# A sparse attention and a gated FFN in one kernel: the written-out order of its work is replaced behind the first FFN product

## The chip, the cores and the metric

The kernel runs on one NeuronCore of a Trainium2 chip. The metric is the device time of one execution in microseconds (us), as the median of several runs. A profile of one further execution shows what each engine did: PE (TensorE, the matrix engine; PEld its weight loads), ACT (ScalarE), DVE (VectorE), POOL (GpSimd) and SP (SyncE, which here only issues transfers).

## What is computed

```python
# q, k, v: 4 batches, 8 heads, 768 positions, 64 per head
k_sum = k.reshape(B, H, nb, block, D).max(axis=3)        # block = 32
v_sum = v.reshape(B, H, nb, block, D).mean(axis=3)
scores_l = scale * np.matmul(q, k.transpose(0, 1, 3, 2)) # kept where |i - j| < 16
scores_s = scale * np.einsum('bhsd,bhnd->bhsn', q, k_sum) + np.log(block)
# softmax over both together, then the weighted sum over v and v_sum
x = attn_out.transpose(0, 2, 1, 3).reshape(B * S, H * D) # 3072 tokens, 512 wide
h = x @ w_in                                             # 512 -> 2048
g = h * np.clip(h + 3.0, 0.0, 6.0) / 6.0
out = g @ w_out                                          # 2048 -> 512
```

## The kernel before

The tokens are cut into eight tiles of 384, numbered s = 2 x batch + half. A tile's x is made by the attention of that half batch; then come the first FFN product (512 -> 2048, in eight pairs of 128 rows), a gate on ScalarE and VectorE, and the second FFN product (2048 -> 512, for three groups of 128 tokens).

All work is cut into some 785 small jobs, and `ORDER` is a text that lists them, one token each. A token names a job as *group.number*, and a letter behind a colon picks ScalarE (A) or VectorE (D) where either can do it. Every engine carries out its own tokens strictly in the order of the text. `Plan.run` walks through the text, gives each job a begin and an end by fixed costs, hands out buffers by them (so the text also decides which buffer a job gets), and puts the jobs of all engines out by their planned begin. Waits between engines are set from what the jobs read and write.

The tokens that matter here:

- `F{s}{c}`: first FFN product of tile s. `.0`, `.1` and `.4`, `.5` are TensorE jobs of four products each (line 928), `.2`, `.6` the ScalarE part of the gate (934), `.3`, `.7` the VectorE part (936). A pair of products holds one of three PSUM tiles `S` until its VectorE part is done.
- `G{s}{t}`: second FFN product of 128 tokens. `.0` to `.3` are TensorE jobs of four products (950), `.4` a copy into one of four output buffers `ot` (517), `.5` the store (964, 965), on SP's queue but for G51. A buffer is free again when its store has landed.
- `s{b}{k}`: scores of batch b (681): a TensorE job, an exponential on ScalarE, a mask on VectorE.
- `u{b}`: sums of v by blocks (752) and the copies that spread them over `vaug`.
- `v{b}{T}`: attention values, in two TensorE jobs of 24 products (841), with a scaling on VectorE behind each. For tiles 2, 4, 5, 6 and 7 the last job, `.6`, is a DMA transpose on SP's queue (854) that writes the tile's x; it is called a *turn* below.
- `K`, `Q`, `V`, `h{b}0` to `h{b}2`, `B`: loads on GpSimd's software DMA queue. `I` and `O` load the weights. The raw K and Q of batches 1 and 2 are transposed by VectorE (`k{b}{p}`, `q{b}{p}`, lines 612 and 618); those of batch 3 by turns on SP's queue (`k3e0`, `k3e1`, `q3x0`, `q3x1`, lines 594 and 603).
- `h{b}{c}{x}` of batch 1: the halo of v, a copy within `vaug` (521).
- `y10`: one copy of two elements on GpSimd that reads tile 2's x. GpSimd does nothing more before that turn has landed.

The two lines that make `y10` what it is:

```python
            if b == 1:
                plan.at(f"y{b}{half}")
                op("POOL", 0.15, lambda: nc.gpsimd.tensor_copy(seen[0:1], xt[s].slot[0:1, 0, 0, 0:2]), r=[xt[s], ("x", s, 0)], w=["seen"])
```

Of the kernel before, what the change touches and what calls it, by code (L numbers as in the profile page):

```python
# [38 lines left out]
K10.0 v00.4 u03.1:A v03.0 v00.5:A v03.3 v02.2 v01.4 v02.3 v03.1 v02.4 I3.0 K12.0 K13.0 v01.5:D F00.0 F00.1 v03.2 v02.5:A
F00.2 F00.3 F00.4 v03.4 K11.0 v03.5 F00.5 v03.6 F01.4 F00.6 v03.7:D F01.5 F01.6 F00.7 F00.8 v03.10 v03.8 F00.9 v03.11:A O0.0  # L40
F02.0 v03.9:A F02.1 F01.7 F02.2 F00.10 F00.11 F00.12 F02.3 F00.13 F01.0 F01.1 O1.0 F10.0 F00.14 F10.1 F01.2 F00.15 F01.3
F10.2 F10.3 F13.4 O2.0 F13.5 F13.0 F13.6 F13.1 F11.4 F13.7 F13.2 Q11.0 F11.5 c.3 F12.0 F13.3 Q13.0 F12.1 F11.6 F11.0 F11.7
Q10.0 F11.1 F12.2 F11.2 Q12.0 F03.0 F03.1 F12.3 F03.2 k13.0 F11.3 F02.4 F02.5 F03.3 F02.6 G01.0 k12.0 F10.4 F10.5 k11.0 G01.1
F12.4 F02.7 F12.5 O3.0 k10.0 F03.4 F03.5 F10.6 F10.7 G10.0 w1.0 w1.4:A w1.3:A F12.6 V12.0 G02.0 G02.1 G02.2 F03.6 V10.0 V13.0
F12.7 F03.7 w1.1 q10.0 q13.0 G11.0 G10.1 q12.0 q11.0 G10.2 G11.1 G01.2 h121.0:D w1.2:A G11.2 h120.0:A q14.0:D V11.0 G11.3
h100.0:D h101.0:D G11.4:A G10.3 h130.0:D h131.0:D s120.0 G10.4:A G11.5 s110.0 s120.1 G02.3 G01.3 G00.0 h21.0 G02.4:A h110.0:D
# [6 lines left out]
F20.1 G31.1 F20.2 G32.1 G32.2 F20.3 F21.0 q21.0 F21.4 q20.0 w2.4:A F21.5 F21.1 F20.4 w2.0 F21.6 F21.2 G31.2 G32.3 q22.0 V20.0
F20.5 G32.4:A F21.7 F20.6 F23.0 F23.1 w2.1 G31.3 w2.2:A F20.7 V22.0 G30.0 F21.3 h22.0 G30.1 F23.2 K31.0 s240.0 F23.3 s230.0
s250.0 G30.2 h30.0 G31.4:A s240.1 F22.0 F22.1 B33.0 G30.3 s250.1 s230.1 F22.2 V21.0 u2.0 q24.0:A s210.0 s220.0 F22.3 s200.0
G30.4:A s210.1 s240.2 s220.1 u2.1:D u2.8:D s250.2 s210.2 u2.2:D u2.9:A u2.4:A s230.2 s220.2 u2.7:D G20.0 F22.4 F22.5 F22.6
# [4 lines left out]
k3e1.0 q3x1.0 G31.5 G20.5 F42.4 F42.5 F42.6 F42.7 F50.0 F50.1 F52.4 F52.5 F50.2 F52.6 F50.3 F52.7 G22.4:D F51.4 F51.5 F50.4
F50.5 F51.6 F51.7 F50.6 F50.7 F43.0 F43.1 F43.2 F53.0 F43.3 w3.0 G41.0 F51.0 F53.1 F53.2 F53.3 F51.1 F53.4 F53.5 F51.2 F53.6
G41.1 w3.1 F43.4 F53.7 F51.3 F43.5 F43.6 F43.7 U3.1 w3.4:D w3.3:D G41.2 F52.0 G40.0 F52.1 G40.1 G41.3 G40.2 G40.3 F52.2
w3.2:D G41.4:D F52.3 G40.4:A s350.0 s300.0 s320.0 s300.1 s320.1 U3.4:A s350.1 u3.7:A u3.6:A G50.0 G50.1 G52.0 G52.1 s310.0
s340.0 s330.0 G52.2 G52.3 G50.2 s310.1 s340.1 u3.4:A u3.2:A s330.1 u3.0:D s300.2 s350.2 s320.2 u3.1:D s310.2 u3.3:D u3.5:D
v33.0 v33.3 G52.4:D G51.0 G51.1 v33.4 v33.1 v33.2 s340.2 v33.5 G42.0 G42.1 G51.2 G51.3 G42.2 s330.2 v30.0 v30.1 v30.2 v30.3
v30.4 v30.5 G42.3 G52.5 G41.5 G22.5 v33.6 F70.0 F70.1 F70.2 G51.4:A F71.0 F71.1 F71.2 G42.4:D v30.6 G51.5 F70.3 F71.3 F71.4
F71.5 F71.6 F71.7 F70.4 F70.5 F72.4 F72.5 F70.6 F70.7 F60.0 F60.1 F63.4 F63.5 G50.3 F60.2 F60.3 F63.6 F72.6 F63.7 F61.0 F61.1
F72.7 G72.0 F61.2 F73.4 F73.5 F73.6 G50.4:A F61.3 F73.7 F72.0 F72.1 F72.2 F72.3 F73.0 F73.1 F63.0 G71.0 F61.4 F63.1 F61.5
F73.2 F73.3 F63.2 F63.3 G71.3 F61.6 F61.7 F62.4 F62.5 F62.0 G71.1 G71.6 F62.6 F62.7 G71.9 G72.1 G71.4 G72.2 G71.7 F60.4 F62.1  # L70
G71.12 G71.13:A F60.5 G72.3 G70.0 G70.1 G70.2 F60.6 F60.7 F62.2 F62.3 G60.0 G60.1 G70.3 G61.0 G71.14 G42.5 G70.4:D G60.2
G72.4:D G70.5 G72.5 G60.3 G60.4:D G60.5 G71.10:D G71.11 G40.5 G50.5 G62.0 G62.1 G62.2 G61.1 G61.2 G61.3 G62.3 G61.4:D G61.5
G62.4:D G62.5 G71.2 G71.5 G71.8 G71.15 G71.16:A G71.17
# [1023 lines left out]
```

## Time and profile before

| | |
|---|---|
| median of three runs | 212.12 us (211.94 to 213.3) |
| the profiled execution | 211.65 us |
| its span, first to last instruction | 209.9 us |
| granted TensorE clock, mean | 0.999 |
| busy: PE, DVE, ACT, POOL | 201.7, 156.0, 110.8, 68.9 us |
| software DMA queue (GpSimd's loads) | 15.47 MB in 99488 packets |
| hardware DMA queue (SP's turns and stores) | 10.06 MB in 18128 packets |

Times in the profile count from the span's start. A row of a timeline gives start, length, engine, line of the kernel, operation, the tiles written and read with their shapes, and how many instructions were merged; a bracket tells how long the engine was idle before and who ended that. TensorE's products overlap, so the sum of their lengths is more than the time that they take; starts are the better ruler. A few products in a hundred have no record.

### The profile page before, as it was taken

How to read it: one execution, taken by the hardware profiler on the slowest of the kernel's cores; microseconds unless marked ns; L12 is line 12 of the kernel's file. 1: busy time of each engine (PE TensorE's matmuls, PEld its weight loads, DVE VectorE, ACT ScalarE, POOL GpSimd, SP SyncE). 2: the span in 40 equal slices, each digit the busy share in tenths (PEclk: the TensorE clock that was granted, in tenths of full speed). 3: DMA queues.
4: the chain of work that ended last, by engine and by line, in shares of the span. 5: the costliest groups of instructions: out<-in, count | busy, mean ns of one | idle time of the engine just before them, and what ended most of it. 6: DMA issues, size and time to landing. Idle time of an engine off the chain costs nothing.

```text
span 209.9 us, 5030 instructions
## 1 busy us (share of the span) xinstructions
PE 201.7 (96%) x2143; PEld 119.1 (57%) x2166; DVE 156.0 (74%) x229; ACT 110.8 (53%) x158; POOL 68.9 (33%) x89
## 2 busy tenths in 40 slices
...
GB/s 143 198 160 189 165 152 131 204 135 152 158 159 157 124 110 199 137 164 160 161 169 38 173 132 208 214 24 0 2 54 174 67 61 0 3 0 62 23 185 182
DMA packets 117638, 25.85 MB, mean 123 GB/s; under 512 B 108368, under 2 KB 114320, under 8 KB 117616
## 3 DMA queue, kind: packets, MB, share of 16 engines
q0 software_dynamic: 99488, 15.47, 106.8%
q1 hardware_dynamic: 18128, 10.06, 20.3%
q8 instruction: 17, 0.28, 0.6%
q14 instruction: 5, 0.04, 0.1%
...
## 4 chain that ended last, share of the span: by engine, by line
PE 60%; DMA 22%; POOL 5%; issue 5%; DVE 5%; ACT 2%; SPq 0%; POOLq 0%; ACTq 0%
PE S L928 28%; PE h L950 19%; PE S L950 9%; DMA vaug<-in_v_dram 9%; DMA wout<-in_moe_w_out_dram 5%; DMA win<-in_moe_w_in_dram 4%; DMA g<-in_q_dram 3%; PE S L841 2%; POOL nat L455 2%; DMA out_dram<-ot 2%; DVE at L689 2%; DVE g L936 1%; PE S L681 1%; DVE vaug L517 1%; ACT at L687 1%
## 5 line engine op out<-in xcount | busy, mean ns | idle before, releaser
L928 PE MATMUL S<-x,win 128*128 128x384 bf16 (+1 forms) x616 | 87.8, 299 | 0.4 <-ACT ot L517 0.3
L936 DVE SCALAR_TENSOR_TENSOR g<-r,S 128x768 bf16<-128x768 f32 x64 | 59.9, 948 | 24.5 <-ACT r L934 24.2
L934 ACT ACTIVATE r<-S 128x768 f32<-128x768 f32 x64 | 51.1, 810 | 46.0 <-PE S L928 42.0
L928 PEld LDWEIGHTS <-win 128*128 128x128 bf16 x616 | 53.6, 98 | 31.6 <-issue 0.8
L950 PEld LDWEIGHTS <-g 128*128 128x128 bf16 x416 | 38.7, 98 | 40.3 <-DVE g L936 0.4
L950 PE MATMUL h<-wout,g 128*128 128x512 bf16 (+2 forms) x256 | 58.6, 362 | 1.5 <-issue 1.0
L950 PE MATMUL S<-wout,g 128*128 128x512 bf16 (+1 forms) x139 | 30.0, 361 | 0.6 <-issue 0.3
L965 POOL DMA_DIRECT2D out_dram<-ot x1 | 0.6, 586 | 59.0 <-ACT ot L517 59.0
L687 ACT ACTIVATE at<-S 120x1024 bf16<-120x1024 f32 x18 | 17.9, 1023 | 1.6 <-PE S L681 1.4
L467 POOL DMA_DIRECT2D vaug<-in_v_dram x16 | 15.2, 949 | 6.4 <-issue 5.7
L517 ACT COPY ot<-h 128x512 f32<-128x512 f32 (+1 forms) x12 | 6.7, 558 | 18.4 <-PE h L950 16.9
L689 DVE TENSOR_TENSOR at<-at,mask 96x1024 bf16<-96x1024 bf16 x18 | 11.7, 683 | 1.6 <-ACT at L687 0.9
L455 POOL DMA_DIRECT2D nat<-in_k_dram x8 | 10.5, 1319 | 6.2 <-issue 4.7
L455 POOL DMA_DIRECT2D nat<-in_q_dram x8 | 10.6, 1329 | 3.3 <-issue 2.7
L782 DVE TENSOR_REDUCE red<-kb 128x48 bf16<-128x1536 bf16 x6 | 10.4, 1738 | 0.0
L517 DVE COPY ot<-S 128x512 f32<-128x512 f32 x5 | 3.5, 690 | 9.0 <-PE S L950 5.8
L517 ACT COPY ot<-S 128x512 f32<-128x512 f32 (+1 forms) x4 | 2.0, 502 | 14.8 <-DMA out_dram<-ot 10.0
L618 DVE STREAM_TRANSPOSE q<-nat 128x768 bf16<-128x768 bf16 x8 | 7.3, 956 | 2.8 <-issue 2.8
L521 DVE TENSOR_TENSOR vaug<-vaug 32x640 bf16<-32x640 bf16 (+2 forms) x21 | 7.7, 409 | 1.6 <-DMA vaug<-in_v_dram 1.2
L517 ACT COPY vaug<-vs 24x768 bf16<-24x768 bf16 x10 | 8.2, 827 | 0.2
L849 DVE TENSOR_TENSOR xm<-S,rc 128x768 bf16<-128x768 f32 x8 | 7.6, 954 | 0.2
L739 DVE TENSOR_REDUCE total<-nat 128x32 f32<-128x1024 bf16 x4 | 7.6, 1897 | 0.0
...
## 6 DMA issues: line engine op xcount, KB each, us to landing
...
wout<-in_moe_w_out_dram POOLq DMA_DIRECT2D x4, 512.0 KB, 11.4
nat<-in_q_dram POOLq DMA_DIRECT2D x8, 192.0 KB, 13.6
...
```

Source lines behind the costliest of these rows:

```text
L455: op("POOL", 1.35, over=0.01, fn=lambda src=src, name=name, hs=hs, ds=ds, rows=rows: nc.gpsimd.dma_start(out=raw[b % 2][name][rows], in_=s ...
L467: op("POOL", 0.945, lambda: nc.gpsimd.dma_start(out=o[BLK:WIN, lo:hi, 0:D], in_=rows[:, lo:hi]), w=[("v", b % 2, c)], dma=1.28, els=1536). ...
L517: {"ACT": nc.scalar.copy, "DVE": nc.vector.tensor_copy, "POOL": nc.gpsimd.tensor_copy}[eng](o, i)
L521: nc.vector.tensor_tensor(o, i, i, op=ALU.max)
L687: op("ACT", 1.02, lambda: nc.scalar.activation(odds[0:KEYS, :, w], X.slot[0:KEYS], AF.Exp, scale=scl), r=[X], w=[("atg", k)])
L689: op("DVE", 0.69, lambda: nc.vector.tensor_tensor(odds[0:WIN, :, w].rearrange("p j (t c) -> p j t c", c=QB), odds[0:WIN, :, w].rearrange(" ...
L739: nc.vector.tensor_reduce(total[:, h * D + lo:h * D + lo + n], x[:, lo:lo + n], axis=AX.X, op=ALU.add)
L782: nc.vector.tensor_reduce(red.slot[:].rearrange("x (p u e n) -> x e u p n", p=NP, u=NS, e=2)[:, e], w[:, n * e:n * e + n, BLK:WIN].rearran ...
L928: nc.tensor.matmul(h.slot[:, f, u * 128:z * 128].rearrange("p (u c) -> p u c", c=128), w_in_sb[:, kt, (ft + f) * 128:(ft + f + 1) * 128], ...
L934: op("ACT", 0.81, lambda: nc.scalar.activation(r.slot[:], h.slot[:, :, 0:HALF], AF.Relu, bias=0.5, scale=1.0 / 6.0), r=[h], w=[r], alloc=r)
L936: op("DVE", 0.955, lambda: nc.vector.scalar_tensor_tensor(gt[s].slot[:, ft:ft + 2], r.slot[:], 1.0, h.slot[:, :, 0:HALF], op0=ALU.min, op1 ...
L950: nc.tensor.matmul(bank(o)[:, a:z], gt[s].slot[:, ft, ts * 128:(ts + 1) * 128], w_out_sb[:, ft, a:z], start=(ft == 0), stop=(ft == NFT - 1))
```

## The change

Only `ORDER` changes, from token 123 of 785 on, which is shortly before the first FFN product. It is a new order of the same jobs: 28 of them go to the other one of ScalarE and VectorE, none is added or left out. The costs in `Plan` are as before. Some stretches of it (each line holds many tokens; lines left out are marked):

```diff
-m.0 s110.1 G01.4:A s100.0 s150.0 s100.1 h111.0:D u1.0 u1.1:A K20.0 u1.6:A Q23.0 K22.0 s130.0 G00.1 G00.2 G00.3 Q21.0 K21.0
...
-v10.0 v10.3 Q22.0 v13.9:D G02.5 v10.1 F30.0 v10.2 F30.1 F30.2 v10.4 v10.5 v10.6 F30.4 F30.5 F31.4 F30.3 F31.5 G10.5 F30.6
-G12.4:A F33.4 G12.5 F30.7 F31.6 F33.5 y10.0 G01.5 F33.6 k21.0 F31.7 F33.0 F33.7 F33.1 h20.0 G31.0 Q32.0 F33.2 V30.0 F32.0
-k20.0 F31.0 F33.3 F31.1 F31.2 k22.0 F32.1 F32.4 k23.0 F32.2 F32.5 F31.3 q23.0 G32.0 F32.6 Q33.0 F20.0 w2.3:A F32.3 F32.7
...
-F23.4 G22.0 F23.5 G20.1 G22.1 F22.7 u2.3:D u2.6:D F23.6 F23.7 s200.1 v20.0 v20.3 s200.2 v20.4 v20.1 u2.5:D v20.2 v20.5 B31.0
-K32.0 Q35.0 h31.0 K35.0 K33.0 Q31.0 V32.0 K34.0 B32.0 B30.0 h32.0 V31.0 Q34.0 Q30.0 V33.0 G21.0 G21.1 G22.2 G22.3 v23.3 v23.0
-G20.2 G20.3 G21.2 G21.3 v20.6 G30.5 G21.4:A U3.2 v23.1 v23.4 U3.3 v23.2 U3.0 v23.5 F40.0 F40.1 F40.2 F41.4 F41.5 F41.6 F40.3
...
+h110.0:D m.0 G00.1 s100.1 s100.2 h111.0:A s110.1 s120.2 u1.0 u1.1:A u1.9:D u1.7:D s110.2 u1.3:D G02.4:A s130.0 K23.0 s150.0
...
+F31.0 F31.1 Q20.0 k21.0 F32.6 F32.3 v10.6 G32.0 F32.7 F20.0 k23.0 F31.2 F21.4 F31.3 w2.0 w2.1 F21.5 K30.0 F20.1 F21.6 F20.2
+F20.3 F21.7 Q22.0 q23.0 h21.0 G32.1 G32.2 w2.3:D V21.0 w2.2:A F20.4 F20.5 G32.3 G32.4:A G32.5 F21.0 q20.0 Q32.0 w2.4:A F20.6
...
+F22.0 G30.4:D u2.2:A Q34.0 F23.6 G22.1 u2.6:A s200.2 k3e0.0 F22.7 u2.7:A G20.0 v20.3 F23.7 v20.0 v20.4 v20.1 v20.2 F22.1
+k3e1.0 F22.2 G20.1 G21.0 v20.5 B30.0 B33.0 F22.3 G21.1 G21.2 G21.3 v20.6 G20.2 G20.3 G21.4:A u2.5:D w3.3:A s220.2 v23.3 G21.5
+B31.0 w3.0 w3.1 v23.0 v23.1 v23.2 G20.4:A F40.0 F40.1 F40.2 v23.4 v23.5 F42.0 F42.1 F42.2 F41.4 F41.5 F40.3 F42.3 F41.6 F41.0
...
+G72.3 G71.6 G71.9 G62.1 G72.4:A G72.5 G71.10:A G60.5 G71.11 G62.2 G62.3 y10.0 G71.2 G71.5 G71.8 G62.4:D G61.4:A G62.5 G61.5
...
```

GpSimd's queue, behind the third input weight, in the two orders (loads by their group names):

```
before  K10 I3 K12 K13 K11 O0 O1 O2 Q11 Q13 Q10 Q12 O3 V12 V10 V13 V11 h21 m K20 Q23 K22 Q21 K21 K23 K30 Q20 V23 Q22
        y10 h20 Q32 V30 Q33 V20 V22 h22 K31 h30 B33 V21 B31 K32 Q35 h31 K35 K33 Q31 V32 K34 B32 B30 h32 V31 Q34 Q30 V33
after   K10 I3 K12 K13 O0 K11 O1 Q13 O2 Q12 Q10 Q11 O3 V12 V13 V10 V11 m K23 K22 K20 Q21 V20 K21 h20 Q30 Q23 V22 K33
        K32 Q20 K30 Q22 h21 V21 Q32 K35 h22 V23 K34 K31 Q31 h30 B32 Q34 B30 B33 B31 h31 Q33 Q35 V32 h32 V31 V30 V33 ... y10
```

SP's queue, from batch 1's values on: before, two stores, the turn of tile 2, the stores of G10, G12 and G01, the turn of tile 4, G30 and G00, the turn of tile 5, then the Q and K turns of batch 3 with stores between them. After: the stores of G01, G12 and G02, the turn of tile 2, the stores of G32, G31, G00 and G11, the two K turns of batch 3 and behind them the turn of tile 4, G21, G30, the turn of tile 5, G20, and the Q turns of batch 3.

More of the change, by code (lines that the diff above doesn't have):

```diff
@@ L38 @@
 u03.0:A h031.0:D u02.1:A h021.0:A I0.0 v01.0 v00.0 v00.1 v01.1 u02.2:D v00.2 I1.0 I2.0 v00.3 v02.0 v01.2 v02.1 u01.1:A v01.3
[L39 to L46, printed above, removed]
@@ L47 @@
-m.0 s110.1 G01.4:A s100.0 s150.0 s100.1 h111.0:D u1.0 u1.1:A K20.0 u1.6:A Q23.0 K22.0 s130.0 G00.1 G00.2 G00.3 Q21.0 K21.0
-s120.2 s100.2 u1.3:D u1.5:D u1.2:D s130.1 u1.7:A u1.9:D s110.2 s130.2 G12.0 v13.3 v13.0 v13.4 s150.1 K23.0 s140.0 v13.1 v13.2
-v13.5 u1.8:A K30.0 Q20.0 s140.1 G12.1 G12.2 v13.6 G12.3 s150.2 u1.4:A v13.7:A V23.0 s140.2 v13.10 v13.8 v13.11:D G00.4:A
-v10.0 v10.3 Q22.0 v13.9:D G02.5 v10.1 F30.0 v10.2 F30.1 F30.2 v10.4 v10.5 v10.6 F30.4 F30.5 F31.4 F30.3 F31.5 G10.5 F30.6
-G12.4:A F33.4 G12.5 F30.7 F31.6 F33.5 y10.0 G01.5 F33.6 k21.0 F31.7 F33.0 F33.7 F33.1 h20.0 G31.0 Q32.0 F33.2 V30.0 F32.0
@@ L52 @@
-k20.0 F31.0 F33.3 F31.1 F31.2 k22.0 F32.1 F32.4 k23.0 F32.2 F32.5 F31.3 q23.0 G32.0 F32.6 Q33.0 F20.0 w2.3:A F32.3 F32.7
[L53 to L56, printed above, removed]
@@ L57 @@
-F23.4 G22.0 F23.5 G20.1 G22.1 F22.7 u2.3:D u2.6:D F23.6 F23.7 s200.1 v20.0 v20.3 s200.2 v20.4 v20.1 u2.5:D v20.2 v20.5 B31.0
-K32.0 Q35.0 h31.0 K35.0 K33.0 Q31.0 V32.0 K34.0 B32.0 B30.0 h32.0 V31.0 Q34.0 Q30.0 V33.0 G21.0 G21.1 G22.2 G22.3 v23.3 v23.0
-G20.2 G20.3 G21.2 G21.3 v20.6 G30.5 G21.4:A U3.2 v23.1 v23.4 U3.3 v23.2 U3.0 v23.5 F40.0 F40.1 F40.2 F41.4 F41.5 F41.6 F40.3
-F41.7 G00.5 v23.6 q3x0.0 F41.0 F41.1 F41.2 F41.3 F42.0 F42.1 F42.2 G20.4:A F42.3 F40.4 F40.5 F40.6 F40.7 k3e0.0 G21.5 G32.5
@@ L61 @@
[L61 to L73, printed above, removed]
+K10.0 v00.4 u03.1:A v03.0 v00.5:A v03.3 v02.2 v01.4 v02.3 v03.1 v02.4 I3.0 K12.0 K13.0 v01.5:D O0.0 K11.0 v03.2 v02.5:A F00.0
@@ new lines @@
+F00.1 F00.2 F00.3 v03.4 v03.5 F00.4 F00.5 O1.0 F01.0 F00.6 F01.1 v03.6 c.3 F02.0 F02.1 F00.7 v03.7:A v03.8 F01.2 F01.3 v03.10
+v03.9:D F02.2 F02.3 F02.4 F02.5 v03.11:A F10.0 F10.1 F12.4 F02.6 F02.7 F10.2 F10.3 F12.5 F12.6 F12.7 Q13.0 F01.4 F01.5 F01.6
+F01.7 F11.4 F11.5 F12.0 F12.1 F11.6 F11.7 F12.2 F12.3 F13.4 F13.5 F13.6 F13.7 F11.0 F11.1 F11.2 F00.8 F00.9 F00.10 F00.11
+F00.12 O2.0 F00.13 F11.3 F03.4 Q12.0 F03.5 Q10.0 F00.14 F00.15 Q11.0 F10.4 k10.0 k13.0 F10.5 F10.6 G01.0 G01.1 F03.0 F03.1
@@ new lines @@
+F03.2 k12.0 k11.0 F10.7 F03.3 w1.0 w1.1 w1.4:A G02.0 G02.1 F03.6 G02.2 F03.7 G10.0 F13.0 F13.1 F13.2 G10.1 w1.2:A F13.3
+w1.3:D q13.0 G01.2 O3.0 q10.0 G11.0 G11.1 G10.2 G11.2 q11.0 V12.0 q12.0 q14.0:D G10.3 G10.4:A V13.0 G11.3 G11.4:A V10.0
+h120.0:D G01.3 G01.4:A h121.0:D h130.0:D h131.0:D V11.0 h101.0:D s120.0 s120.1 s100.0 s110.0 G02.3 G00.0 G01.5 h100.0:D
+h110.0:D m.0 G00.1 s100.1 s100.2 h111.0:A s110.1 s120.2 u1.0 u1.1:A u1.9:D u1.7:D s110.2 u1.3:D G02.4:A s130.0 K23.0 s150.0
+s150.1 s150.2 s140.0 G00.2 u1.6:D K22.0 G12.0 u1.5:A G00.3 K20.0 v13.0 Q21.0 s130.1 v13.1 v13.2 s140.1 s140.2 u1.2:A v13.3
```

19 lines of the change are left out of this document (added).

## The prediction

> **What bounds the kernel now.** I read the page's busy line first, then the chain that ended last, a table of stretches from 30 to 200 us, and TensorE's list of waits.
>
> ```profile
> span 209.9 us, 5030 instructions
> ...
> PE 201.7 (96%) x2143; PEld 119.1 (57%) x2166; DVE 156.0 (74%) x229; ACT 110.8 (53%) x158; POOL 68.9 (33%) x89
> ...
> PE 60%; DMA 22%; POOL 5%; issue 5%; DVE 5%; ACT 2%; SPq 0%; POOLq 0%; ACTq 0%
> ...
> sum 170.00, PE 167.18 PEld 96.19 DVE 129.22 ACT 88.92 POOL 51.06; mean PE 18.57 PEld 10.69 DVE 14.36 ACT 9.88 POOL 5.67
> ...
> PE S L928 <- ACT ot L517: 0.3, 1, 0.3
> ...
> PE S L752 <- DVE vaug L521: 0.3, 1, 0.3
> ...
> PE S L950 <- DVE g L936: 0.2, 1, 0.2
> ```
>
> TensorE is the bound: it is busy for 201.7 of 209.9 us and holds 60% of the chain. The row "sum" adds nine stretches from 30 to 200 us: 167.18 busy of 170.00. So behind the head a new order can win at most 2.82 us, 1.3%, and only if it leaves TensorE no idle moment at all. The list of waits names 0.8 us of that: 0.3 for a copy of an output tile, 0.3 for a halo in `vaug`, 0.2 for a gate. The rest are gaps that no other engine's work ends.
>
> Before the first FFN product the order stays, and behind the last one it can move little: the last accumulation is in both orders 128 columns wide, followed by one copy and one 64 KB store.
>
> **The frame of the sum.** The profiled execution took 211.65 us, 1.75 more than its span, and lies 0.47 under 212.12, the median of the three runs shown. I sum against 211.65 and add 0.47 at the end. About 1% (2.1 us) is what a measurement of this kernel can tell from no change.
>
> **What the change leaves alone.** It permutes tokens, and of 28 copies and similar jobs it hands 13 from ScalarE to VectorE and 15 back; neither engine is the bound, so I price the swap at 0 except where it is named below. I counted TensorE's jobs from v03.0 on: 282 in each order, the same ones, with 25 switches between FFN and attention products in each. So TensorE's own work is worth 0, and an instruction of the new order is placed by counting which jobs have moved across it. That needs two prices:
>
> ```profile
> 117.14 1.89 PE L950 MATMUL S<-wout,g 128*128 128x512 bf16 x8
> 118.87 1.46 PE L928 MATMUL S<-x,win 128*128 128x384 bf16 x8
> ...
> 120.66 13.81 PE L928 MATMUL S<-x,win 128*128 128x384 bf16 x84 [0.32 <-ACT ot L517]
> 134.31 1.03 PE L950 MATMUL h<-wout,g 128*128 128x512 bf16 x3
> ```
>
> These are rows of TensorE's timeline: start, length, engine, line, operation, tiles, count, and in brackets the idle time before. Lengths overlap, so I take starts. Eight second-FFN products take 118.87 - 117.14 = 1.73 us, so a G job of four costs 0.86. The 84 first-FFN products take 134.31 - 120.66 = 13.65, so an F job of four costs 0.65.
>
> **What it wins.** At 120.66 TensorE waits 0.32 for a ScalarE copy that waits for a free output buffer. When that copy (G20.4) comes in the old order, all four buffers are held and stores stand behind a turn in SP's queue; in the new order only three are. Gone: -0.3. The two other waits lie where batch 1's attention begins:
>
> ```profile
> 57.13 0.93 PE L681 MATMUL S<-q,kb 64*128 64x64 bf16 x32
> ...
> 60.69 0.64 PE L681 MATMUL S<-q,kb 64*128 64x64 bf16 x32
> ...
> 61.75 0.85 PE L752 MATMUL S<-vaug,ind 96*32 96x128 bf16 x47 [0.26 <-DVE vaug L521]
> ...
> L467 POOL DMA_DIRECT2D vaug<-in_v_dram x1: 942/942/942, 48.0 to 48.0; - x1
> ...
> DMA to landing us min/median/max: 12.6/12.6/12.6
> ```
>
> The same 32 score products take 0.93 and then 0.64, so 0.29 of waiting hides in the first group. The new order puts one more G job (G01.3, 0.86) ahead of them: -0.3. The sum u1.0 waits 0.26 for the last halo, cut from a load (V11) that lands at 48.0 + 12.6 = 60.6. The same loads stand ahead of V11 in both orders, but the new one lets ScalarE copy one of the two late halos beside VectorE and reaches u1.0 about half a microsecond later by count: -0.3. Together **-0.9**. This term lies between 0, if each wait only moves, and -2.8, if every gap closes; I take the three that I can name.
>
> **What it may cost.** TensorE's jobs are moved for nothing, but the transfers get other company. The token y10.0 made GpSimd wait for the turn (the DMA transpose) of tile 2's x before it issued more loads; it now stands last.
>
> ```profile
> 71.41 1.31 POOL L455 DMA_DIRECT2D nat<-in_q_dram  x1
> 81.96 0.18 POOL L858 COPY seen<-x 1x2 bf16<-1x2 bf16 x1 [9.24 <-DMA x<-xm]
> ...
> 74.34 1.38 SPq L854 DMA_TRANSPOSE x<-xm  x1
> ...
> DMA to landing us min/median/max: 7.6/7.6/7.6
> ...
> 84.42 1.46 PE L928 MATMUL S<-x,win 128*128 128x384 bf16 x8
> ...
> DMA to landing us min/median/max: 13.7/13.7/13.7
> ```
>
> GpSimd issued nothing for 9.24 us, the turn went out at 74.34 with only older loads still moving, and landed after 7.6, at 81.9. Its reader F20.0 starts at 84.42: 2.5 us to spare. The same number of jobs stands ahead of F20.0 in the new order, so after the 0.6 won before it 1.9 are left. Without the hold, loads of V, K and Q keep coming through the turn. The nearest row for a transfer in such company is the load issued at 71.41, whose landing took 13.7 (the last row); at that, x would land at 88.0 and F20.0 start 4.2 late. The other end is 7.6 again, 0 late. The turn is the same kind of transfer as in the 7.6 row, and that one was loaded half of its way: I take 9, which the spare covers: **0**.
>
> The second turn is that of tile 4's x. There the company changes more.
>
> ```profile
> 109.86 0.96 PE L841 MATMUL S<-vaug,at 120*64 120x65 bf16 x48
> ...
> 114.06 1.43 SPq L854 DMA_TRANSPOSE x<-qwide  x1
> ...
> DMA to landing us min/median/max: 4.0/4.0/4.0
> ...
> L467 POOL DMA_DIRECT2D vaug<-in_v_dram x1: 951/951/951, 107.1 to 107.1; - x1
> ...
> DMA to landing us min/median/max: 6.2/6.2/6.2
> ...
> 105.66 0.35 DVE vaug L517
> ```
>
> In the old order the values of that tile start at 109.86, the turn is issued 4.20 later and lands in 4.0, and F40.0 starts at 118.87, 9.01 after the values: 0.8 to spare. The last software load (V33) was issued at 107.1 and landed at 113.3, so this turn ran alone. In the new order one F job stands between the values and F40.0 where a G job stood: 9.01 - 0.21 = 8.80. VectorE does one copy of 0.35 less in between: turn after 3.85. Landing in 4.0, it would leave 0.95 to spare; landing in 7.6, it is 2.65 late, and TensorE, which takes its jobs in order, stands still for that.
>
> Is it alone? The values come earlier: F22.1 and G20.1 have moved behind them (1.5 us), and 0.6 was won before, so the turn is issued near 114.06 - 1.5 - 0.6 - 0.35 = 111.6. The software loads gain the time of the hold, but SP now sends two K turns (landing in 5.0 below) and more stores ahead of it, and the four B loads, which wait for batch 2's transposes, stand ahead of the last V loads:
>
> ```profile
> L603 SPq DMA_TRANSPOSE kb<-nat x2: 1700/1960/2220, 124.9 to 129.1; - x2
> ...
> DMA to landing us min/median/max: 4.8/5.0/5.2
> ...
> 78.00:84.00 6.00, 5.89 (x59) 4.19 (x60) 5.74 (x7) 2.93 (x5) 1.87 (x3) 1.00 0.96 182
> 84.00:90.00 6.00, 6.00 (x32) 3.03 (x32) 4.70 (x6) 3.10 (x5) 6.00 (x8) 1.00 2.17 140
> ```
>
> The DMA share (last but one column) is 0.96 in the hold's stretch against 2.17 after it, so at most 6 x (2.17 - 0.96) / 2.17 = 3.3 us come back; the K turns and the stores cost about as much. The loads would end near 113, 2 us either way: after the turn's issue, likely. I take a landing halfway between 4.0 and 7.6, 5.8: 0.85 late, **+0.8**.
>
> The Trainium skill ("DMA: Bandwidth & Descriptors", "Queues, rings and completion order") says that each DMA engine takes turns packet by packet between the queues that have work. The 7.6 against 4.0 agrees in kind: slowed, not shut out. By equal shares the part behind the issue would double (1.43 + 2 x 2.6 = 6.6), an estimate from that rule, and the sum would be 0.9 higher.
>
> For places with under 0.3 us of spare I add **+0.2** (0 to 1): above all F02.0, which comes some 0.8 earlier, at about 26.2, while its weights land at 25.9 (GpSimd sees them at the first row's time):
>
> ```profile
> 26.00 0.18 POOL L1054 COPY seen<-win 1x2 bf16<-1x2 bf16 x1 [1.37 <-DMA win<-in_moe_w_in_dram]
> ...
> q8 instruction: 17, 0.28, 0.6%
> ```
>
> TensorE's instructions arrive in 17 packets (q8). No wait of TensorE above is put down to them, so knowing of them in the plan is worth 0.
>
> **Sum:** -0.9 + 0 + 0.8 + 0.2 = +0.1; 211.75 by the profiled execution, **212.2** as a median.
>
> **The rivals.** (A) *Every transfer is in time*: the 0.8 falls away and little of the 0.2 is left. -0.9 gives 211.2; closing all gaps would give 209.3. For it: both turns have spare time when they land as before. Against: the spare at F40.0 is 0.95 only.
>
> (B) *Slower: the turns wait behind the software queue*. Places: F20.0 and F40.0. F40.0 then costs 2.65 and F20.0 about 1.9 (a landing of 11.4, between 9 and 13.7), so -0.9 + 2.65 + 1.9 + 0.2 = +3.85, 216.0; F40.0 alone gives +1.95, 214.1. It decides from a landing of 5.0 us at F40.0 and of 10.1 at F20.0. For it: 7.6 was measured with loads moving for half the turn. Against: the end of the loads may come before 111.6.
>
> (C) *VectorE takes over as the bound*:
>
> ```profile
> L618 DVE STREAM_TRANSPOSE q<-nat 128x768 bf16<-128x768 bf16 x8 | 7.3, 956 | 2.8 <-issue 2.8
> ...
> 110.00:114.00 4.00, 3.78 (x61) 2.17 (x60) 3.94 (x8) 0.03 (x1) 0.00 (x0) 1.00 0.78 48
> ```
>
> It is already busy 3.94 of 4.00 us from 110 to 114. The new order puts V20, h20, Q30, V22, K33, K32 and K30 ahead of batch 2's last Q load, which landed at 71.4 + 13.7 = 85.1. Four transposes of 0.96 and some 3.5 us of gates must follow it before the scores s230 near 97.5: from a landing of 90 on each microsecond is lost. A landing of 91.5 costs 1.5: 213.7.
>
> (D) The change finds nothing to win and loses nothing: 212.1, inside the forecast's own range.
>
> **Chances.** Forecast with D 0.45 (211.5 to 213.2), A 0.28 (209.3 to 211.5), B 0.17 (213.5 to 217), C 0.10 (212.5 to 215). Faster by over 1% means under 210.0: only A's far end, 0.04. Slower by over 1% means over 214.2: most of B and a little of C, 0.17. Within 1%: 0.79. The range leaves out A's last third of the way and B's upper half, about 0.15 together: 210.5 to 214.9.
>
> **What would show it.** In the changed kernel's TensorE timeline: no bracket at u1.0 and none from an output copy near F41 (the -0.9); a bracket, or a lengthened first F4 product, of about 0.8 us near 117 to 118, released by the turn (the +0.8); no bracket ahead of F20.0 near 84; turn landings of about 9 and 5.8. TensorE's idle between 30 and 200 us should again be near 2.8. I am wrong if a wait of over 2 us stands at F40.0 or F20.0, if VectorE waits for a raw Q load after 90, or if idle there falls under 1.5.

## The result, and the profile after

| | before | after |
|---|---|---|
| median, us | 212.03 (211.11 to 213.3, 6 runs) | 220.5 (218.2 to 221.21, 6 runs) |
| ratio to before | | 1.039, 95% interval 1.0331 to 1.0448 |
| profiled execution, us | 211.65 | 220.38 |
| its span, us | 209.9 | 218.6 |
| granted TensorE clock, mean | 0.999 | 0.975 |

The new order is 8.5 us slower; 212.2 was forecast, with 210.5 to 214.9 as the range. In this section and the next, medians are over all runs of a kernel, while ratios leave out executions over 1.5% above its fastest (a few took 299 to 1172 us, two of them of the kernel before).

From the page of the kernel after: the busy line and the chain that ended last. Then TensorE's list of waits, whole.

```profile
span 218.6 us, 5061 instructions
PE 206.7 (95%) x2166; PEld 120.1 (55%) x2166; DVE 155.1 (71%) x227; ACT 112.0 (51%) x160; POOL 69.2 (32%) x89
PE 79%; DMA 13%; ACT 4%; DVE 2%; issue 1%; DVEq 0%; ACTq 0%
```

```profile
PE S L928 <- DMA x<-qwide: 7.5, 1, 7.5
PE h L1052 <- PEq L1081: 0.8, 1, 0.8
PE S L928 <- DVE g L936: 0.3, 1, 0.3
```

One row holds nearly all of it. `x<-qwide` is the turn of tile 4's x, and its reader is F40.0. TensorE's timeline shows the wait, and the table of stretches what followed (columns: stretch, length, busy PE, PEld, DVE, ACT and POOL with counts, granted clock, DMA share, GB/s).

```profile
115.95 0.95 PE L841 MATMUL S<-vaug,at 120*64 120x65 bf16 x48
124.36 8.36 PE L928 MATMUL S<-x,win 128*128 128x384 bf16 x36 [7.45 <-DMA x<-qwide]
132.56 1.03 PE L950 MATMUL h<-wout,g 128*128 128x512 bf16 x4
```

```profile
116.00:120.00 4.00, 0.91 (x49) 0.79 (x48) 0.36 (x1) 0.36 (x1) 1.06 (x2) 0.86 1.64 143
120.00:124.00 4.00, 0.00 (x0) 0.00 (x0) 3.58 (x5) 1.04 (x3) 0.00 (x0) 0.50 1.87 170
124.00:128.00 4.00, 3.64 (x12) 1.80 (x13) 0.00 (x0) 0.80 (x1) 0.00 (x0) 0.50 1.87 215
128.00:132.00 4.00, 4.00 (x23) 2.23 (x22) 2.56 (x4) 1.63 (x3) 0.00 (x0) 0.86 1.33 208
...
sum 170.00, PE 162.21 PEld 91.89 DVE 126.26 ACT 86.45 POOL 51.31; mean PE 16.22 PEld 9.19 DVE 12.63 ACT 8.64 POOL 5.13
```

TensorE stands still for 7.45 us. Within the pause its granted clock falls to 0.50, and it stays there until past 128. The 36 products from 124.36 to 132.56 take 8.20 us; 36 of the same, behind a short wait, take 5.85 at full clock (127.06 to 132.91 in e4 below; e5's rows give 6.15, but there one of the four products behind, most likely the first, has no record). So the lower clock costs 2.35 more. 7.45 + 2.35 = 9.8, against 8.7 us of longer span: the rest of the order won 1.1 in this execution. The row "sum" shows the one wait again: of 170.00 us from 30 to 200, 7.79 are idle, 7.45 of them there.

Why x came late is read on SP, GpSimd and VectorE. Timeline rows first, then the landings of these transfers (last row of the view of their line):

```profile
100.17 11.68 SPq L603 DMA_TRANSPOSE kb<-nat  x2
111.95 5.40 SPq L854 DMA_TRANSPOSE x<-qwide  x1
```

```profile
113.68 0.58 POOL L493 DMA_DIRECT2D vaug<-in_v_dram  x1 [9.33 <-DMA vaug<-in_v_dram]
114.25 2.82 POOL L467 DMA_DIRECT2D vaug<-in_v_dram  x3
```

```profile
119.64 1.75 DVE L782 TENSOR_REDUCE red<-kb 128x48 bf16<-128x1536 bf16 x1 [4.08 <-DMA kb<-nat]
```

```profile
L603 SPq DMA_TRANSPOSE kb<-nat x2: 4913/5759/6605, 100.2 to 106.9; - x2
...
DMA to landing us min/median/max: 12.7/13.1/13.6
```

```profile
L854 SPq DMA_TRANSPOSE x<-qwide x1: 5397/5397/5397, 112.0 to 112.0; - x1
...
DMA to landing us min/median/max: 12.4/12.4/12.4
```

```profile
L467 POOL DMA_DIRECT2D vaug<-in_v_dram x3: 942/942/951, 114.2 to 116.1; - x3
DMA to landing us min/median/max: 11.1/11.5/12.0
```

The turn went out at 111.95, as forecast (111.6), and landed after 12.4 instead of 4.0. The two K turns just ahead of it took 12.7 and 13.6 (4.8 and 5.2 before). On GpSimd the small load h32 writes beside h31 and waits for its landing, 9.33 us, so the last four loads left between 113.7 and 116.1, on top of the turn, and ended at 116.1 + 12.0 = 128.1; before they ended at 113.3.

### The profile page after: what moved, and what is told of

Its sections match the earlier page's. It is cut to its first block, busy times and chain, and to the rows that moved or that the text cites. A ratio compares the mean times of both kernels' runs of the same rounds, so it can differ in the third digit from the quotient of the medians.

```text
span 218.6 us, 5061 instructions
## 1 busy us (share of the span) xinstructions
PE 206.7 (95%) x2166; PEld 120.1 (55%) x2166; DVE 155.1 (71%) x227; ACT 112.0 (51%) x160; POOL 69.2 (32%) x89
## 4 chain that ended last, share of the span: by engine, by line
PE 79%; DMA 13%; ACT 4%; DVE 2%; issue 1%; DVEq 0%; ACTq 0%
PE S L928 35%; PE h L950 23%; PE S L950 9%; DMA x<-qwide 6%; DMA kb<-nat 5%; PE h L1052 3%; DMA out_dram<-ot 2%; PE S L681 1%; ACT vaug L517 1%; ACT at L687 1%; PE S L841 1%; PE S L646 1%; PE h L573 1%; PE S L810 1%; PE h L702 1%
## 5 line engine op out<-in xcount | busy, mean ns | idle before, releaser
L928 PE MATMUL S<-x,win 128*128 128x384 bf16 (+1 forms) x616 | 90.6, 304 | 7.8 <-DMA x<-qwide 7.5
L928 PEld LDWEIGHTS <-win 128*128 128x128 bf16 x616 | 54.2, 99 | 41.2 <-DMA x<-qwide 7.6
L950 PE MATMUL h<-wout,g 128*128 128x512 bf16 (+1 forms) x304 | 67.3, 362 | 0.0
L950 PE MATMUL S<-wout,g 128*128 128x512 bf16 (+1 forms) x112 | 23.9, 364 | 0.0
L517 ACT COPY ot<-S 128x512 f32<-128x512 f32 (+1 forms) x6 | 3.3, 550 | 17.4 <-PE S L950 14.7
L521 DVE TENSOR_TENSOR vaug<-vaug 32x768 bf16<-32x768 bf16 (+2 forms) x20 | 7.6, 422 | 1.3 <-DMA vaug<-in_v_dram 0.6
L517 DVE COPY ot<-S 128x512 f32<-128x512 f32 x1 | 0.7, 693 | 10.3 <-PE S L950 10.3
L841 PEld LDWEIGHTS <-at 120*64 120x64 bf16 x336 | 6.2, 111 | 2.4 <-issue 1.7
```

Source lines behind the costliest of these rows:

```text
L517: {"ACT": nc.scalar.copy, "DVE": nc.vector.tensor_copy, "POOL": nc.gpsimd.tensor_copy}[eng](o, i)
L841: nc.tensor.matmul(X.slot[64 * c:64 * c + 64, e, (D + 1) * y:(D + 1) * (y + 1)], odds[0:KEYS, j, u * QB:(u + 1) * QB], vaug[b % 2][0:KEYS, ...
L928: nc.tensor.matmul(h.slot[:, f, u * 128:z * 128].rearrange("p (u c) -> p u c", c=128), w_in_sb[:, kt, (ft + f) * 128:(ft + f + 1) * 128], ...
L950: nc.tensor.matmul(bank(o)[:, a:z], gt[s].slot[:, ft, ts * 128:(ts + 1) * 128], w_out_sb[:, ft, a:z], start=(ft == 0), stop=(ft == NFT - 1))
```

## The experiments

The theories as they were written down: K, the K turns ahead make the turn late; S (later L), the loads that run through it do; KL, each slows the other. Tables give median, ratio to the kernel before with its 95% interval, and the landing of tile 4's turn.

**First set: take away one or the other.**

e1 and e5 (the same kernel; e1's profiled execution was the one of 1172 us, so e5 gives the trace): both K turns behind tile 5's turn, and what VectorE makes of them later.

```diff
-s200.2 k3e0.0 F22.7 ... F22.1 k3e1.0 F22.2 ... u2.5:D w3.3:A s220.2 ... B31.0 w3.0 w3.1 v23.0
+G22.2 v23.6 k3e0.0 k3e1.0 Q33.0 ... F53.3 w3.0 ... F40.7 w3.1 ... F43.7 w3.2:D w3.3:A w3.4:A
```

> The new order with batch 3's two K turns moved behind the turn of tile 5 in SP's queue, and VectorE's work on them (w3) as much later. Theory K (the turns of K in front of tile 4's x turn, in the same queue, make it late): its landing falls from 12.4 to at most 6 us, the wait at F40.0 from 7.5 to under 1, the time to 211 to 212.5 us. Theory S (GpSimd's software loads, which now run through it, make it late): the landing stays at 10 us or more, the wait at 4 or more, the time over 216. If both share it, the landing is 7 to 9 and the time 213 to 215.

> The same kernel as e1: both K turns behind the turn of tile 5's x, the software loads where the changed kernel has them. Wanted from it is the trace. Theory L (the loads that run past 112 make the late turn, the K turns ahead of it add little): the landing of tile 4's turn stays over 9 us, F40.0 waits 4 us or more and the clock falls. Theory K (the two K turns ahead make it): the landing falls to 4 to 6, F40.0 waits under 1.5 us. Theory KL (each slows the other): the K turns gone, h31 lands earlier, the last loads go out earlier, and the landing comes out between, 6 to 9. Time 213 to 215.5 by K and KL, over 217 by L.

e2: GpSimd waits for tile 4's turn before it sends h31 and the seven loads behind it; e3: e1 and e2 together.

```diff
-            if b == 1:
+            if b == 1 or b == 2 and not half:
                 plan.at(f"y{b}{half}")
...
-G21.5 B31.0 w3.0 w3.1
+G21.5 B31.0 y20.0 w3.0 w3.1
```

> The new order, K turns where they are, but GpSimd waits for the turn of tile 4's x before it issues the loads h31, Q33, Q35, V32, h32, V31, V30 and V33 (one copy of two elements, as y10 did for tile 2). Theory S: landing of that turn at most 6 us, wait at F40.0 under 2, time 211 to 213. Theory K: the landing stays at 9 us or more and the time over 216. Under either the K turns land earlier than 113.8 and 119.6 if the loads slowed them.

> Both edits: K turns behind, loads held. Both theories: the turn of tile 4's x lands in about 4 us, as when it ran alone before (4.0); no wait at F40.0; TensorE's clock at 1.00 throughout. What is left of the new order then shows: 211.2 us if the 0.9 us forecast as won is real, 212.1 if nothing was won. A wait further on, for batch 3's loads or K turns, would show as idle before s35 or F50.

e4: 34 idle products of 512 columns on TensorE ahead of F40.0, so that it is busy while it waits.

```diff
+        if o.key == "F40.0":
+            todo.append(lambda s=o.alloc[0].slot: keep(34, s))
         todo.append(o.fn)
```

> The new order with 34 idle products of 512 columns (7.3 us, into the bank that F40.0 takes next) put before F40.0, so that TensorE does not stand still while it waits. The theory that the wait of 7.5 us costs a further 2.2 us through the lowered clock behind it (0.5 from 120 to 128): the clock stays at 1.00, the first F4 and F5 jobs take 0.65 and not 1.28, and the time falls by 2.2 to about 218. If the slow jobs behind the wait have another cause (weights, transfers), the time stays at 220.5.

| | median, us | ratio | landing, us |
|---|---|---|---|
| after | 220.5 | 1.039 (1.0331 to 1.0448) | 12.4 |
| e1 | 214.87 | 1.010 (1.0057 to 1.0143) | |
| e5 | 214.5 | 1.0091 (1.0046 to 1.0136) | 4.9 |
| e2 | 214.35 | 1.0059 (1.0016 to 1.0102) | 3.6 |
| e3 | 218.85 | 1.0235 (1.0174 to 1.0297) | 3.7 |
| e4 | 219.86 | 1.0365 (1.0286 to 1.0445) | 13.4 |

e5: the last row of the view of tile 4's turn, and TensorE's timeline. e2: the same for tile 4's turn, then F50.0 in TensorE's timeline and the landing of tile 5's turn, for which it waits.

```profile
DMA to landing us min/median/max: 4.9/4.9/4.9
```

```profile
117.65 6.10 PE L928 MATMUL S<-x,win 128*128 128x384 bf16 x36
123.80 0.81 PE L950 MATMUL h<-wout,g 128*128 128x512 bf16 x3
```

```profile
DMA to landing us min/median/max: 3.6/3.6/3.6
```

```profile
129.80 1.47 PE L928 MATMUL S<-x,win 128*128 128x384 bf16 x8 [2.50 <-DMA x<-xm]
```

```profile
DMA to landing us min/median/max: 7.5/7.5/7.5
```

For tile 4's turn either removal alone is enough: with the loads running but no K turns ahead, 4.9; with both K turns but the eight loads held, 3.6. It takes both to make it late, as KL has it, though each landing lies where K or S alone had put it and under the 6 to 9 written down for KL. Neither kernel is back at the time before. In e2 the held loads burst out when tile 4's turn lands and meet tile 5's (7.5 instead of 3.8 before), and F50.0 waits 2.50; that is read in an execution of 216.62 us, one of e2's longer ones, and how much of it the shorter ones have is not known. e3 is worse than either: K turns and held loads now start together around tile 5's turn. In its profiled execution (219.9 us, the longest of four) F50.0 waits 3.4 for that turn, and gates and scores wait 1.7 behind VectorE (TensorE's waits in e3):

```profile
PE S L928 <- DMA x<-xm: 3.4, 1, 3.4
PE S L928 <- DVE g L936: 1.0, 2, 0.5
...
PE S L681 <- DVE g L936: 0.7, 2, 0.5
```

e4 settles the clock, in its table of stretches and in TensorE's timeline:

```profile
124.00:128.00 4.00, 3.18 (x17) 1.47 (x15) 1.27 (x3) 0.00 (x0) 0.00 (x0) 1.00 2.00 225
```

```profile
127.06 6.01 PE L928 MATMUL S<-x,win 128*128 128x384 bf16 x36 [0.82 <-DMA x<-qwide]
132.91 1.03 PE L950 MATMUL h<-wout,g 128*128 128x512 bf16 x4
```

The clock stays at 1.00 and the 36 products take 5.85 instead of 8.20. The median hardly fell all the same: in the profiled execution x landed at 127.0 instead of 124.3, since the turn left 1.65 later (113.60) and took 1.0 longer. So the 2.35 is shown as a part of the profiled loss, not as a gain in the time.

**Second set: how much of each, and a repair.** e6 has two holds: h31, Q33 and Q35 wait for tile 4's turn, the last five loads for tile 5's. e7 has only the second hold. e8 has none, but h31 earlier.

```diff
 # e6 and e7 (b == 1 or b == 2 and half)
-            if b == 1:
+            if b in (1, 2):
-G21.5 B31.0 w3.0 ... F40.6 V32.0
+G21.5 B31.0 y20.0 w3.0 ... F40.6 y21.0 V32.0
 # e8
-s250.2 h30.0 G11.5 ... F43.0 w3.2:D h31.0 F41.7
+s250.2 h30.0 h31.0 G11.5 ... F43.0 w3.2:D F41.7
```

> The changed kernel with two holds: GpSimd waits for tile 4's turn before h31, Q33 and Q35, and for tile 5's turn before the last five loads (V32, h32, V31, V30, V33). The K turns stay ahead. By theory L both turns land in about 4 to 5 us, neither F40.0 nor F50.0 waits over 1 us, the clock stays, and the time is that of the kernel before or a little less: 210.5 to 212.5. By a theory that the K turns ahead cost by themselves, F40.0 still waits over 2 us. If the loads come too late now, a new wait stands at the scores of batch 3 (s350, s310) or at v33, and the time is over 213.

> The changed kernel with one hold: the last five loads (V32, h32, V31, V30, V33) wait for tile 5's turn; h31, Q33 and Q35 go out over the K turns as in the changed kernel. If the last five loads are what slows tile 4's turn, its landing is 4 to 6 and the time that of e6. If the three 3 KB-grained loads in flight with the K turns suffice (h31 landed at 113.1, Q35 at 118.6 in the changed kernel), the landing stays at 7 to 9, F40.0 waits 2 to 4 us, and the time is 213.5 to 216.

> The changed kernel with the load h31 moved ahead of B32, right behind h30; no hold. In the changed kernel h32 waits on GpSimd for h31's landing (9.3 us of waiting, 103.8 to 113.1), and so the last four loads go out at 113.7 to 116.1, on top of tile 4's turn. If that chain is what put them there, they go out near 104 to 108 now, the loads end near 119 to 121 instead of 128, and the landing of tile 4's turn falls to 7 to 10: F40.0 waits 2 to 5 us, time 214 to 218. If the landing depends on the amount of loads and not on their place, the wait stays over 6 us and the time near 220.

| | median, us | ratio | landing, us |
|---|---|---|---|
| e6 | 214.11 (210.62 to 218.05) | 0.9993 (0.9947 to 1.0039) | 3.6 |
| e7 | 217.69 | 1.026 (1.0213 to 1.0308) | 8.5 |
| e8 | 221.88 | 1.043 (1.0368 to 1.0492) | 11.5 |

TensorE's timeline of e7 and of e8, and GpSimd's of e8:

```profile
121.87 7.70 PE L928 MATMUL S<-x,win 128*128 128x384 bf16 x36 [3.06 <-DMA x<-qwide]
```

```profile
124.89 5.39 PE L928 MATMUL S<-x,win 128*128 128x384 bf16 x24 [6.15 <-DMA x<-qwide]
```

```profile
105.08 0.68 POOL L493 DMA_DIRECT2D vaug<-in_v_dram  x1
```

Three loads beside the two K turns make 8.5, all eight 11.5 to 13.4. In e8 the last loads did leave from 105 on, as the chain over h31 said, and it helped nothing: by these traces it counts how much is in flight with the K turns, not when it was issued. e6's ratio rests on its 5 shortest executions of 12, and its median lies above them: in the profiled one (218.05, the longest) F50.0 still waited 2.6 for tile 5's turn, now beside h31, Q33 and Q35.

**Third set.** e9 is e6 with work put ahead of the reader of tile 5's x; e10 is e5 with the last five loads held; e11 is the kernel before with only y10 moved to the end; e12 is the kernel after with one K turn ahead instead of two.

```diff
 # e9
-v23.6 Q33.0 U3.3 F43.1 F50.0 G20.5 F50.1 F41.3 w3.4:A Q35.0 F43.2 F43.3 G22.3 F50.2
+v23.6 Q33.0 U3.3 F43.1 F41.3 w3.4:A Q35.0 F43.2 F43.3 G22.3 G20.5 F50.0 F50.1 F50.2
 # e10, on e5: y21.0 ahead of V32.0, U3.3 behind U3.2
 # e11, on the order before
-F33.5 y10.0 G01.5 ... G62.3
+F33.5 G01.5 ... G62.3 y10.0
 # e12: k3e1.0 behind v23.6, w3.1 behind F40.7, w3.2 to w3.4 behind F43.7
```

> The kernel with two holds (e6), and the first products that read tile 5's x (F50.0, F50.1) moved behind F41.3, F43.2, F43.3, G22.3 and G20.5: some 3.7 us of TensorE's work. In e6 F50.0 waited 2.6 us for tile 5's turn, which the three released loads slowed to 7.6. If that wait is all that keeps e6 from its best, it goes, and the time is 210 to 211.8 in most runs. If the late start of F50 only moves the wait to a gate or to the scores of batch 3, the time stays at 213 to 215.

> K turns behind tile 5's turn as in e5, the last five loads held until tile 5's turn has landed, and the sum U3.3 moved behind U3.2 to free VectorE. If tile 4's turn then meets only h31, Q33 and Q35, it lands in 4 to 5; tile 5's turn lands in about 4 instead of 5.2 and F50.0 waits for nothing (0.55 in e5); the waits for gates of e5 (0.5 + 0.7) shrink with the sum moved. Time 211 to 212.5, against 214.5 of e5. If the K turns and the five loads, now started together near 122, slow each other as they did in the changed kernel, the copies of K come late and the scores of batch 3 wait 2 us or more: 213.5 to 216.

> The kernel before, with only GpSimd's wait for the turn of tile 2's x moved to the end: all loads behind it may go out up to 9 us earlier. The prediction priced this at 0: tile 2's turn lands in 9 instead of 7.6 and F20.0 does not wait. If so, the time is that of the kernel before within 0.5%, and the loads end about 3 us before 113. If the turn lands in over 10.1, F20.0 waits and the time is 1 to 4 us more. Its trace shows too whether TensorE loses 1 to 2 us by 70 us, as it did in most traces of the changed order: by the theory that this comes with the order, it does not here.

> The changed kernel with one K turn ahead of tile 4's turn and the other behind tile 5's. With two ahead that turn landed in 12.4, with none in 4.9. If the K turns and the loads slow each other in proportion, it lands in 7 to 9 and F40.0 waits 2 to 3.5 us; time 214 to 217. If it is the number of transposing transfers in flight that counts (the second starts before the first has landed, and the third before the second), one alone ahead is done before tile 4's turn starts: landing 5 to 6, F40.0 waits under 1 us, time 212.5 to 214.5.

| | median, us | ratio | landing, us |
|---|---|---|---|
| e9 | 211.89 (210.58 to 214.39) | 0.999 (0.9953 to 1.0026) | 3.6 |
| e10 | 217.79 | 1.0275 (1.0227 to 1.0323) | 3.7 |
| e11 | 211.42 | 0.9983 (0.9956 to 1.0011) | 4.0 |
| e12 | 214.63 (one run) | | 6.8 |

Two rows of e12 (the landing of tile 4's turn, TensorE's timeline), e10's longest wait, the landing of tile 2's turn in e11 and in e9, and what F20.0 waited for it in e9:

```profile
DMA to landing us min/median/max: 6.8/6.8/6.8
```

```profile
119.87 6.03 PE L928 MATMUL S<-x,win 128*128 128x384 bf16 x36 [1.30 <-DMA x<-qwide]
```

```profile
PE S L681 <- DMA q<-nat: 3.7, 1, 3.7
```

```profile
DMA to landing us min/median/max: 9.3/9.3/9.3
```

```profile
DMA to landing us min/median/max: 11.2/11.2/11.2
```

```profile
PE S L928 <- DMA x<-xm: 0.7, 1, 0.7
```

With the loads running, the landing grows with the K turns ahead: none 4.9, one 6.8 (a single run, and between the two landings expected), two 11.5 to 13.4. e9 wins back all that the change lost and ties with the kernel before; its ratio rests on 11 of 12 executions. e10 moved the same collision once more: K turns and last loads leave close together, from 120.5 on, the Q turns behind them land in 11.0 and 9.6, and the scores wait 3.7.

**Fourth set: what in the K turns does it.** e13 sends K of batch 3 as plain copies of the same bytes (not transposed, so its scores are not the reference's). e14 is e9 with y10 back, ahead of h21. e15 has ScalarE issue tile 4's turn, in a queue of its own; e16 does that with the `w3` jobs placed as in e5. e17 is e13 with the two copies issued by ScalarE, one right behind the other.

```diff
 # e13 (e17: nc.scalar, and the jobs on ACT)
-nc.sync.dma_start(out=kb[i][:, n * e:n * e + n, BLK:WIN], in_=..., transpose=True)
+nc.sync.dma_start(out=kb[i][64 * e:64 * e + 64, :, BLK:WIN], in_=...)
 # e14
-Q22.0 q23.0 h21.0 ... G62.3 y10.0
+Q22.0 y10.0 q23.0 h21.0 ... G62.3
 # e15, e16
-            op("SP", 1.3, lambda: nc.sync.dma_start(out=xt[s].slot[:]...
+            by = ("ACT", nc.scalar) if (b, half) == (2, 0) else ("SP", nc.sync)
+            op(by[0], 1.3, lambda: by[1].dma_start(out=xt[s].slot[:]...
```

> The changed kernel with batch 3's two K turns issued as plain copies of the same bytes in the same places of SP's queue (K of the last batch is copied, not transposed). If what slows tile 4's turn is the bytes of the two transfers ahead, it still lands in 10 us or more and F40.0 waits over 5 us: 218 to 221. If it is that they transpose (the form of the transfer), they land in 5 to 8, tile 4's turn in 4 to 6, as without them, the loads go out as in e5, and the time is 213 to 215.

> The kernel with two holds and the later F50 (e9), and GpSimd's wait for tile 2's turn back, ahead of h21 (behind Q22). In e9 that turn landed in 11.2 us and F20.0 lost 0.9. With four loads held (h21, V21, Q32, K35) it should land in 8 to 9.5, F20.0 loses nothing, h21 lands sooner after its issue, and the time is 0.3 to 0.9 under e9: 210.8 to 211.7, ratio to the kernel before 0.994 to 0.999. If the held loads come too late for batch 2's values (V20 to V23) or for the K turns, a new wait stands near 90 to 112 and the time is that of e9 or more.

> The changed kernel with one instruction on another engine: ScalarE issues the turn of tile 4's x, so that it no longer stands behind the K turns in SP's queue. K turns, stores and loads go out as in the changed kernel, and the same bytes move. Theory Q (SP's queue is served in order, and what stands ahead sets the landing: in all traces x landed 4 to 6 us after the transfer ahead of it): it lands in 4 to 7, F40.0 waits under 1.5 us and the clock stays up. Tile 5's xm still comes late, because VectorE waits for the second K turn at 119.6, so F50.0 waits 2 to 4 us: time 213.5 to 216. Theory B (the bytes in flight, whatever their queue, slow every transfer): it lands in 9 or more, F40.0 waits over 4 us, 217 to 221.

> As e15, with the five jobs that need the K turns' results placed as in e1 and e5 (the first reduction behind F53.3, the second behind F40.7, the copies behind F43.7), so that VectorE does not wait for the K turns ahead of tile 5's scaling. By theory Q tile 4's x is in time, tile 5's turn goes out near 120, F50.0 waits under 1.5 us, and the gates wait about 1.5 us as in e5: 212 to 214. By theory B F40.0 still waits over 4 us: 217 or more.

> As e13 (batch 3's K is copied in plain copies, not transposed), but ScalarE issues the two copies, one right behind the other, so that they travel in a queue of their own; the turn of tile 4's x stays in SP's queue, now with only stores ahead. In e15 the turn could not tell the theories apart: on ScalarE's queue it went out only at 121.2, when the second K turn had landed (the program makes a turn of another queue wait for the turns before it). Theory Q (the place behind the K transfers in SP's queue makes it late): x lands in 5 to 7.5 as in e5, F40.0 waits under 2.5 us, 213 to 216.5. Theory B (the bytes in flight slow it, whatever their queue): it lands in 10 us or more, F40.0 waits over 5 us, 217 to 223. A landing between, 8 to 9.5, would say that each has a part.

| | median, us | ratio | landing, us |
|---|---|---|---|
| e13 | 224.3 (2 runs) | 1.0596 (1.0537 to 1.0656) | 16.2 |
| e14 | 212.5 | 0.9997 (0.9957 to 1.0037) | 4.0 |
| e15 | 223.44 | 1.052 (1.0433 to 1.0608) | 7.0, from 121.2 on |
| e16 | 224.61 | 1.0603 (1.0551 to 1.0656) | 6.0, from 122.0 on |
| e17 | 229.78 (2 runs) | 1.0797 (1.0664 to 1.093) | 11.5 |

The turn's landing in e13 and in e17, TensorE's two longest waits in e17, and ScalarE's timeline in e15:

```profile
L858 SPq DMA_TRANSPOSE x<-qwide x1: 10708/10708/10708, 111.4 to 111.4; - x1
...
DMA to landing us min/median/max: 16.2/16.2/16.2
```

```profile
L858 SPq DMA_TRANSPOSE x<-qwide x1: 2807/2807/2807, 112.4 to 112.4; - x1
DMA to landing us min/median/max: 11.5/11.5/11.5
```

```profile
PE S L932 <- DVE xm L853: 8.6, 1, 8.6
PE S L954 <- DVE g L940: 4.9, 1, 4.9
```

```profile
112.30 0.81 ACT L935 ACTIVATE r<-S 128x768 f32<-128x768 f32 x1 [1.19 <-PE S L929]
121.17 1.38 ACTq L855 DMA_TRANSPOSE x<-qwide  x1
122.64 0.59 ACT L517 COPY ot<-S 128x512 f32<-128x512 f32 x1 [9.53 <-issue]
```

Plain copies make it worse, so the K transfers need not transpose to make the turn late. e15 and e16 missed their aim: the program lets a turn from another engine start only when the turns before it have landed, here the second K turn at 121.0, and x became later. The Trainium skill ("DMA: Bandwidth & Descriptors", "Silent corruption: two transposing streams in flight at once") says that software must keep such turns apart; the trace shows its price: ScalarE stands still from 113.1 to 121.2. e17 answers in part: in SP's queue only stores stood ahead of the turn, the K copies travelled in another, and it still took 11.5. So company in another queue can make it late. e17's longer time is another matter: F40.0 does not wait for the turn there, because TensorE is late already (4.9 at a gate, while ScalarE issues the copies), and F50.0 waits 8.6 for VectorE, which waits for K. Whether the place in the queue adds to it (16.2 in e13) stays open, because e17's copies also left 7 us later. And copies are no exact stand-in for turns: from 96 to 130 us e13 moves 22728 packets, the kernel after 21066.

So a rival stays for the real turns: that tile 4's turn waits in SP's queue until the K turns ahead of it are through, and that the loads slow them all. In the kernel after, 7.7 of its 12.4 us pass before the second K turn has landed (at 119.6) and 4.7 behind that, close to e5's 4.9. In no trace with K turns ahead does it land before the last of them: 4.0 to 5.7 us behind where all the loads run (after, e4, e8, e12), 1.3 to 2.2 behind where some or all are held (e2, e6, e7, e9, e14), so the 4 to 6 of e15's expectation holds for the first group alone. That K turns and loads together make it late is shown; by which of the two ways is not.

## Why the prediction was wrong

**The step that failed** is the landing of tile 4's turn: "I take a landing halfway between 4.0 and 7.6, 5.8", +0.8. It measured 12.4, and TensorE stood for 7.45. Both ends came from turns with less company: none, and older loads for half of the way. For tile 2's turn the prediction had quoted 13.7 for a load in the full stream and used it as an end; for tile 4's it did not, though that is nearly what came.

Behind it stand two smaller steps. That "the K turns and the stores cost about as much" took a K turn as a bit of engine time (landing 5.0); with loads beside it one took 12.7 to 13.6. "The loads would end near 113, 2 us either way": they ended at 128.1. The prediction saw the B loads ahead of the last loads, but not that h32 waits for h31, and not that h31 lands so late (12.8, issued at 100.33, landed at 113.1). The K turns are the smaller part of that: without them h31 still takes 10.7 (e5).

**A term was missing.** No case counted that a TensorE that idles for microseconds comes back slower: 2.35 us here. The Trainium skill states it ("TensorE: Matmul & The Clock Gate", "Part 1: The HAM clock gate"): after an idle window of about 3.4 us the clock falls to half until TensorE has been busy about as long. The trace agrees in kind: 0.50 after 7.45 idle. In time it differs: if the clock is only ever 1.00 or 0.50, the 0.86 of 116 to 120 and of 128 to 132 put the fall at 118.9, 2.0 us into the pause, and the return at 129.1, 4.8 after TensorE resumed. Already a wait of 3.06 (e7) stretched the 36 products to 7.70 us; one of 1.30 (e12) did not (6.03), and with one of 2.50 (e2) the mean clock stayed at 0.999.

**The gains were right in size, in this execution.** Forecast -0.9; outside the wait and the clock it won 1.1. At u1.0 and at the scores the brackets are gone, as they are at the output copy (TensorE's timeline of after; the third row is F20.0, for further below):

```profile
58.18 0.87 PE L681 MATMUL S<-q,kb 64*128 64x64 bf16 x48
...
61.68 1.04 PE L752 MATMUL S<-vaug,ind 96*32 96x128 bf16 x48
```

```profile
84.37 2.76 PE L928 MATMUL S<-x,win 128*128 128x384 bf16 x16
```

They are no sure gain, though. Other executions of the same head lost more at u1.0 (TensorE's waits in e7, the first row), and the old order in e11 lost 0.9 at the scores (the second):

```profile
PE S L752 <- ACT vaug L517: 1.2, 1, 1.2
```

```profile
PE S L681 <- DVE q L517: 0.9, 1, 0.9
```

With the transfers repaired, e9 and e14 tie with the kernel before (0.999 and 0.9997); 0.4% of gain lies at the edge of their intervals and is not shown. The +0.2 for places with little spare came out at 0.3 (a gate); F02.0, named for it, waited for nothing here, but 0.85 for its weights in e12.

**The y10 hold at 0 was right within 0.7, with some luck.** Tile 2's turn was taken as 9 and landed in 9.4; F20.0 (its row at 84.37 has no bracket) waits for nothing. But the 15 other traces of this order (e2 to e10, e12 to e17) have 9.7 to 11.5, and in nine of them F20.0 starts late, by up to 0.7. In the old order its removal changes nothing (e11, 0.9983, landing 9.3). The point given, 10.1, does not follow from the prediction's own spare of 1.9, which gives 7.6 + 1.9 = 9.5; e9, with a landing of 11.2 and a wait of 0.7, puts it at 10.5. Putting the hold back behind Q22 (e14) brought no time, and the turn still landed in 11.2 instead of the 8 to 9.5 expected.

**The idle bound** of 2.82 us was partly no idle time: the profile before has records of 2143 products and the one after of 2166, for the same jobs, and after has 0.34 idle beside its one wait. So the sign "idle there falls under 1.5" could not have told right from wrong.

**Rival B** named the place, the engine and part of the reason (the software queue, not the K turns), and the sign "a wait of over 2 us stands at F40.0" is what came. Its price, 2.65 late and 214.1, had the same wrong end of 7.6 in it; at F20.0 its 1.9 did not come. No case's range reached 220. Priced with 13.7, F40.0 comes 13.7 - 4.0 - 0.95 = 8.75 late, and B at F40.0 alone gives 220.2. That this is so near 220.5 is luck: a landing 1.3 too long stands in for part of the missing clock. Rival C did not come: VectorE's waits in the kernel after have none for a raw load of Q.
